# Token and channel mixer behind a retention block: two transposes moved to the crossbar, a last chain cut in halves, GpSimd scaling a few tiles, and a new fixed order of the work

## The chip, the core and the metric

The kernel runs on one core of a Trainium2 chip. A core has a matrix engine (TensorE, PE in the profile; its weight loads are shown apart as PEld), a vector engine (VectorE, DVE), a scalar engine (ScalarE, ACT), a general engine (GpSimd, POOL) and an engine that here only issues transfers (SyncE, SP). The engines run their own instruction streams and wait for one another through semaphores. Products land in eight banks of PSUM; ACT and DVE empty them into the on-chip memory (SBUF). Time is the device time of one launch in microseconds (us). The kernel before took 187.42 us, the median of 3 runs (186.85 to 187.65).

## The reference

Two parts follow each other. The first is a recurrence over 768 steps for 4 batches of 8 heads with 64 channels:

```python
gamma = 1.0 - 2.0 ** (-5.0 - np.arange(H))          # one decay for each head
scale = 1.0 / np.sqrt(D)
for t in range(S):
    state = gamma[None, :, None, None] * state + np.einsum('bhd,bhe->bhde', k[:, :, t], v[:, :, t])
    y[:, :, t] = scale * np.einsum('bhd,bhde->bhe', q[:, :, t], state)
```

With heads side by side, y is x of the second part, 4 x 768 x 512. That part mixes along the 768 steps and then along the 512 channels:

```python
xt = x.transpose(0, 2, 1)
h  = np.maximum(xt @ w_tok1, 0.0) @ w_tok2           # 768 -> 256 -> 768
u  = x + h.transpose(0, 2, 1)
h2 = np.maximum(u @ w_ch1, 0.0) @ w_ch2              # 512 -> 1536 -> 512
return u + h2
```

Inputs and output are 32-bit floats; the kernel multiplies in 16 bits.

## The kernel before

The 768 steps are cut into 6 chunks of 128, the 8 heads into 4 pairs. The recurrence is computed by chunk: inside a chunk as masked scores times v, between chunks through a state of 64 x 64 for each head.

`front(b, p)` (L501) does one pair of one batch up to u. GpSimd issues the loads of q, k and v (L489, L492), which change type on the way; k of the very first pair comes by SP instead (L492, tile `us`) and in 32 bits. Then:

- `decayed` (L524 to L538) scales k by a factor for each position, one instruction for each head of the pair, on ACT or DVE; for batches 2 and 3 it does the same with q.
- `turn` (L540 to L570) brings k and q to channels on the rows. In mode `t` PE transposes six chunks of 128 x 128 (L554) and one engine copies the bank out; in mode `w` PE does it head by head on half the columns of its array (also L554) and DVE scales on the way out; in mode `x` SP issues one crossbar transpose from SBUF to SBUF (L544).
- PE makes the state products of five chunks (L586) into one bank. DVE takes the first out as it is (L596) and chains the other four (L598). The chained states U are scaled into `cross`, one instruction for each head (L603 to L620).
- PE makes the scores (L637), DVE multiplies them with the causal mask into `am` (L648), PE multiplies `am` with v (L668) and q with `cross` into the same bank (L694). ACT or DVE casts the result to 16 bits (tile `x`, L710).
- Token mixer: PE multiplies with the first weight (tile `wt` of 128x6x256, called wt1 here, L725), ACT or DVE applies the ReLU (L734), PE adds the product with the second weight (two tiles of 128x2x384, wt2, L745) to the bank that still holds x. That is u. It is cast to 16 bits (tile `u`) and kept in 32 bits (tile `X`), both by L710.
- u is turned too, in mode `t` by PE with a copy by ACT or DVE (L790 and L796) or in mode `x` by SP (L780).

The table `TURNS` holds the modes of k, q and u for the 16 pairs: `twt` for the 8 pairs of batches 0 and 1, `xxx` for those of batches 2 and 3.

`back(b)` (L807 on) is the channel mixer. `widen` (L824, batch 0) makes the 1536 hidden channels in the plain way. `widen7` (batches 1 to 3) cuts both operands in two by two blocks and makes the product from seven block products instead of eight (L893); ACT copies partial sums out (L904), DVE adds them up (L913) and applies the ReLU in place (L917, tile `h`, 54 times). `narrow7` does the second product likewise (L1043, L1053), with DVE adding the results to `X` (L1060) and SP or ACT storing rows of 512 columns (L1086); `narrow` (L969, L978, L984) does what is left of batch 3 in the plain way. For the block sums DVE prepares differences of the weights and of the operands (L1007 among others).

PE can treat its 128 x 128 array as a whole, or as halves by rows (scores, L637) or by columns (state products, L586; mode `w`, L554). Matmuls of the three kinds alternate in the order.

The order is written out: `ORDERED` is a string in which two characters of base 62 name one operation, 1296 of them, and `WAYS` is a string with the choice of engine for each operation that has one. `arrange` (L111) goes through this order with a cost model, but only to give the operations banks and buffers and to place a few multiplications by zero (L1168) where it expects PE to be idle at the start. The instructions of every engine, the transfers issued by GpSimd, SP and ACT among them, stand in that order. An engine takes its own in order, so an instruction that waits holds up all behind it on that engine.

Of the kernel before, what the change touches and what calls it, by code (L numbers as in the profile page):

```python
# [9 lines left out]
FP = mybir.dt.float32  # L10
F16 = mybir.dt.float16
AF = mybir.ActivationFunctionType
# [26 lines left out]
class Rings:  # L39
# [12 lines left out]
    def land(self, q, op, t):  # L52
        if q == "POOL":
            return 1470 if t < 4500 else 2100 if t < 17000 else 1700
        if op.dma[0] == 48:
            return 1300 if t < 115000 else 900
        return 900
# [49 lines left out]
INTO, OUT_OF = 92, 111  # L107
FREE = dict(PE=300, ACT=2500, DVE=900, POOL=900, SP=750)


def arrange(ops, BANKS, seq, ways):  # L111
# [82 lines left out]
    while left:  # L194
        moved = False
        wake = INF
        for e in ENGINES:
# [18 lines left out]
            if e == "PE":  # L216
                if o.tiled != tiled:
                    s_ = max(t, free[e] + (INTO if o.tiled else 0) + (OUT_OF if tiled == "high" else 0))
                tiled = o.tiled
# [39 lines left out]
    "0b05040a07000d0103020e060c1e0h1f1i0f1j1g1h0j08090g1t1k1x1s1l0i1O1m1w1P1n1v0l1Q1o1u1S1R1p1y1T0o1z1q1U1r1V221W"  # L259
    "230n2o1A1X242p1Y0m1C1Z2q26202s272r1B2t0k1D2Y252C2D2Z0q2F2u212H302v2G28312a2w292E0r2b2c1E2x2y0t2I2z1F2d342A35"  # L260
    "0p2B1J362e37380s2K1G2f2M2J392L1H2g3a0w2N321I1K2j332h2O0v2i1L3c2P4K0A2k3e3d3b2Q3f2m3h0u2R2T2l3g3i3k1M2U3m3j3l"
    "0z2V1N5j3n3C4L3y3o2S0y3z2W2n3p3A47483q2X0x3t5k3r493u3E3B0E3s3w3vac3xaf3F3GaM3HaN3DadaPaO0Dagaear4aaxah3IaQ0C"
    "3Jas3Mat4baR3Pb73Qb8b13Nau0B3Oavb24cawaD3KaJ0Gayb3aGb9aKazao0F3L4laLaH4oap4n0L4daq3R3TaI4eaA1a3VaBaS4H4GaT4f"
    "ai4maUaj0H4gaE4pak4I4hal4i4J1bbjamaFaVbkan1d3SaC0JbaaWbm3Ubbbo3Wb4aXaYbnb5bc1caZ4jbg0Nb0bd16bh3Xbi0K17b6be3Y"
    "bqbl18bf0I3Z4UbI40bObr19410R424k4Y4M5fbvbP4V4r4t4Nbw4q6p4sbx4X0M4u4Obz4v4Pby43154Wbs5Obp45bA4Q44bBbJ5gbt4w46"
    "4RbKbE4xbL4SbTbCbF4T4Z50bU4y5P0T5152bD4z5Q5l5U4A5m4B0O535V5h5W4CbX5n5X540Pc44DbM5o5ibY555Y5pbNc56mc85q5Z56bR"
    "bu6qc65r575R5Sc95t5sbS5T5a585vcd6n5ubV6r5wce605y5x5AchbQ5C6oc7bW5z5Bci5b0Q6s6Uc06t5D594E5c0U6ucmc17s6v6V5E6w"
    "12cn4F6xcfbZ5F0S617t62cg5G6y640W5J5H665dcj655K145I635e5Mck68670X5N69ca6bcl5L6a0Vcb6A6ccqcu6X6C6d6Y6DcNcc6Z6e"
    "cLcrcvcwcM6B6f6z6WczcscQcxcA6icRct707u6gcCcOcTcD6EcBcUcScycocEcJ806GcV6I6jd0716hcKcGd1cXcH81d26FcY6kdR116H72"
    "d3d4cW736Jd9cZ74d7dS13d5dT6KdWd8d6dU7y7vda757zdX6L7AdbcFcPdZ767Bdcdhe0dY7w6Mde7C0Z7xdie1e683djcI7De3dfe76N6l"  # L270
    "e4dk78dV77dAdd7cdoc2dB6Q7bcp6OdC7982dpdFe5dq6RdDdldG7adrdIdEdsdm7e7gdJdHdt6S86dn84dydK7d7f87dzdP850Y886PdMdL"
    "89ey7hdu8adQe26TdNdv7ieWdg8yeu7j7EdwbGez8bc3eUeX7kev8B7Gew8C7l7K7FeDeQ8zeFdOdxeE7I8A7oeV7meGeHex7peJeS8c7reR"
    "7qeAeI7J7nf1eB8D96eK7M7O7HeMeLbHeZeNf27L7Nf0eC8e107Pe8f37Q8i99f58ff48h7R9a8g8dee9be97Secf697ef9E7TeY8jea8k7U"
    "7Wf7ed8m7V8Eeg9c7XeTej9H7Z9d8F7Y8l9eeh8G9f8Hf898ekeieb8nen8I8of9el9g8J9h8peoemfc8Mep8q8Keq8O8L8r8Qfg8P8s8uer"
    "fx8t8Nfh9kfdfyfi8v9nflfjfCfmfz9mfD8Sfofe8wfO9lfpfF9F8R9ofvfGfA8U9G8Tfn9ifffE8VfqfMfwg58xfH8Wfs9IfN9Kft9jfJ9J"
    "8X9Lfkg6fKfQ9MfP8Ygaetfug7fRgbfT9N9qgdfU9O9p9PeO9r8Zg8gegc9Q90fW9t9s92fX9ufVgfgk91g3fY93ghfIg4g0fBgi949vglg1"
    "gD9w9SgEg2fSgmgg9R9UgIgn9xg9fZgFgJ9Tgr9y9VgLgsgtfrgGgMgKgu9z9W9XgN9ZgvgSgogwgTgBa19AgxgOgCgPfLgp9YgyhChIhEa0"
    "hGgza2gjhNhDhHgQa3gqgHhLhOa4hg9BhRhM9DhFa5hPhJa6hifbgYhSgRhrgAhQhha8hUhTa9hkhsabgUhvgVgZa7h095hK9Ch3hlh1hjfa"
    "hmh4gWePhphnh2h5hqhogXh7h6hth8hVh9huhwhchxhyhahYi2hZiAhbi3ijaai4hdi7ikhei0ilesi8i5iohAi9hzipiahWimhfiqhXi1ir"
    "ibiHisicihiTitiiieivifiRiwiCiBj8iSiFiYiDiGiWiUhBiyi6iIiXidjaixiziJiZjfiKj0kEiPiMj1iQj6iNj3jpj2j9j4koj7jdjbjq"  # L280
    "jrinjejwjujsjgjvkMkNkpjhjciEjxiVjtjniLjyjKiujojEigjik6jFjzjkjjkqjAjlkFkOkwk2kPkQkGjBk3k7kriOjCkRksjmkbk4jDkt"
    "j5kcjGkdjHjLkHkIkfkejIjPkSkujMjJkvjRjNkTk5khjQkgjSjTkijVkjjUkJkxkmjWjYjOkKk8jXkLkyjZkzk0k9kAk1kBkkkakCklkDkn"
)
WAYS = (
    "000000000000000000000000000000000000000000000000000000000000000000000000000010000000000000000000000000000010"
    "010100000000000000000000000001010000000100000000000000000000000000000000000100000000000010000000000010000000"
    "000101010000000000000000000000000000000010100000000000000000000000000000001000000000000000000000000000010100"
    "000000000000001000000000000000000001010110000000000000000000000000000000010000000000000000000000000000000000"
    "000000000000000000000000000000010010000000000000000000000000000000000000000000000000000000000000000000000000"
# [11 lines left out]
def kernel(  # L301
# [104 lines left out]
    def emit():  # L406
        for h in range(H):
            nc.vector.memset(lgs[:, h:h + 1], math.log(1.0 - 2.0 ** (-5.0 - h)))
# [792 lines left out]
```

## Time and profile before

| | before |
|---|---|
| time, median of 3 runs | 187.42 us (186.85 to 187.65) |
| time of the profiled execution | 186.83 us |
| its span | 185.0 us |
| granted clock of PE (1 is full) | 0.996 |
| PE busy | 177.1 us |
| PE's weight loads busy | 134.6 us |
| DVE busy | 170.2 us |
| ACT busy | 133.4 us |
| POOL busy | 53.6 us |

The span is what the profile sees, from the first instruction to the last; the time of the same execution is 1.8 us longer. In groups of instructions a row gives line, engine, operation, output and input by the program's names, the shape (partitions x elements), the count, then after the bar the busy time in us and the mean in ns of one, and last the idle time of the engine ahead of them with what ended most of it. In the chain of work that ended last, a row gives the start, the length, the engine and what it did; the chain is followed backwards from the last instruction, at each step to what released it or to the instruction ahead on the same engine. In the rows of transfers stand the tile, the queue, the count, the size of one and the median us from issue to landing.

### The profile page before, as it was taken

Reading aid. Unit: us, or ns where it says so; the run is one execution under the profiler, and the core shown is the slowest. Engines: PE = TensorE matmul, PEld = TensorE weight load, DVE = VectorE, ACT = ScalarE, POOL = GpSimd, SP = SyncE. Lnnn points to the kernel's source line nnn. Section 1 sums busy time; section 2 is a strip of 40 time slices with the busy share of each in tenths; the row PEclk is TensorE's granted clock in tenths of the full one; section 3 lists DMA queues with packets and bytes.
Section 4 is the critical chain, followed back from the end, with each engine's and each line's share of the span. In section 5 each row is a group of like instructions: output and inputs, shape, how many; then the busy total and the mean of one; then the engine's idle time right before and its main releaser. Section 6 shows DMA issues by size and latency. Waiting matters only on the chain.

```text
span 185.0 us, 5291 instructions
## 1 busy us (share of the span) xinstructions
PE 177.1 (96%) x2089; PEld 134.6 (73%) x2089; DVE 170.2 (92%) x466; ACT 133.4 (72%) x304; POOL 53.6 (29%) x63
## 2 busy tenths in 40 slices
PE   7788899999999999999999999999999999999991
PEld 3456788656689988866668898667679986567881
DVE  4599799859999999999999999999999999999992
ACT  5689698469789899999999697898864416552120
POOL 8994786355424609704220020000000000000000
PEclk9999999999999999999999999999999999999998
DMA  6999999999999999999999995027002444500035
GB/s 117 143 160 176 199 170 198 194 189 206 167 157 154 121 156 123 156 148 185 146 233 161 190 138 100 4 43 198 3 0 40 123 143 174 225 0 0 4 142 198
DMA packets 92248, 24.91 MB, mean 135 GB/s; under 512 B 81984, under 2 KB 89280, under 8 KB 92224
## 3 DMA queue, kind: packets, MB, share of 16 engines
q0 software_dynamic: 67728, 13.18, 89.8%
q1 hardware_dynamic: 23056, 9.11, 25.4%
q10 hardware_dynamic: 1440, 2.29, 3.3%
q8 instruction: 16, 0.26, 0.6%
q14 instruction: 8, 0.07, 0.1%
HBM read 26.74 MB, written 6.29 MB: 179 GB/s over the span
## 4 chain that ended last, share of the span: by engine, by line
PE 69%; DVE 16%; POOL 6%; DMA 5%; issue 2%; ACT 1%; POOLq 0%
PE bank L893 18%; PE bank L1043 11%; PE bank L824 9%; PE bank L1053 9%; DMA wt<-in_moe_w_tok_dram 5%; PE bank L745 5%; PE bank L725 4%; DVE X L1060 4%; DVE am L648 4%; DVE hs L1007 3%; PE bank L969 3%; DVE h L913 2%; POOL v L492 2%; PE bank L668 2%; PE bank L637 2%; PE bank L694 2%
## 5 line engine op out<-in xcount | busy, mean ns | idle before, releaser
L648 DVE TENSOR_TENSOR am<-bank,mask 128x384 f16<-128x384 f32 x64 | 32.9, 547 | 2.9 <-PE bank L637 2.8
L913 DVE TENSOR_TENSOR h<-bank,us 128x384 f16<-128x384 f32 x54 | 28.8, 551 | 0.6 <-PE bank L893 0.2
L904 ACT COPY us<-bank 128x384 f32<-128x384 f32 x50 | 23.3, 489 | 8.3 <-PE bank L893 6.4
L492 POOL DMA_DIRECT2D v<-in_v_dram x16 | 16.5, 1034 | 40.4 <-PE bank L694 25.7
L893 PE MATMUL bank<-hs,late 128*128 128x384 f16 x108 | 22.6, 326 | 0.0
L1033 ACT COPY us<-bank 128x256 f32<-128x256 f32 x30 | 10.7, 373 | 14.5 <-PE bank L1043 9.5
L1043 PEld LDWEIGHTS <-hs 128*128 128x128 f16 x198 | 18.5, 98 | 2.4
L893 PEld LDWEIGHTS <-late 128*128 128x128 f16 x144 | 13.2, 98 | 8.2 <-issue 0.4
L1060 DVE TENSOR_TENSOR X<-X,bank 128x256 f32<-128x256 f32 x44 | 17.7, 412 | 0.8 <-PE bank L1053 0.4
L1043 PE MATMUL bank<-wsum,hs 128*128 128x256 f16 x132 | 17.5, 273 | 0.0
L598 DVE SCALAR_TENSOR_TENSOR U<-U,gp,bank 128x64 f32<-128x64 f32 x64 | 16.8, 274 | 0.7
L710 ACT CAST u<-bank 128x384 f16<-128x384 f32 x31 | 14.6, 487 | 3.9 <-PE bank L745 3.3
L824 PE MATMUL bank<-uT,wc 128*128 128x384 f16 x96 | 16.9, 326 | 0.0
L492 POOL DMA_DIRECT2D k<-in_k_dram x15 | 15.4, 1033 | 4.9 <-DVE am L648 1.4
L710 ACT CAST x<-bank 128x384 f16<-128x384 f32 x30 | 14.1, 483 | 3.6 <-PE bank L694 3.4
L893 PE MATMUL bank<-uT,wc 128*128 128x384 f16 x72 | 16.4, 326 | 0.1
L616 ACT ACTIVATE cross<-U,gp 64x320 f16<-64x320 f32 x29 | 16.2, 559 | 0.4
L745 PE MATMUL bank<-h,wt 128*128 128x128 f16 x192 | 15.7, 219 | 0.3 <-DMA wt<-in_moe_w_tok_dram 0.3
L530 ACT ACTIVATE k<-k,gk 128x384 f16<-128x384 f16 x25 | 14.9, 617 | 1.4 <-DMA k<-in_k_dram 1.1
L840 ACT ACTIVATE h<-bank 128x384 f16<-128x384 f32 x24 | 10.6, 492 | 5.0 <-PE bank L824 4.8
L710 ACT COPY X<-bank 128x384 f32<-128x384 f32 x29 | 14.0, 492 | 0.0
L745 PEld LDWEIGHTS <-wt 128*128 128x128 f16 x192 | 12.3, 98 | 2.2 <-DMA wt<-in_moe_w_tok_dram 0.5
(91 smaller groups left out, 382.8 us busy)
## 6 DMA issues: line engine op xcount, KB each, us to landing
out_dram<-X SPq DMA_DIRECT2D x15, 256.0 KB, 3.1
q<-in_q_dram POOLq DMA_DIRECT2D x16, 192.0 KB, 8.4
v<-in_v_dram POOLq DMA_DIRECT2D x16, 192.0 KB, 7.3
k<-in_k_dram POOLq DMA_DIRECT2D x15, 192.0 KB, 7.9
wc<-in_moe_w_ch_dram POOLq DMA_DIRECT2D x5, 512.0 KB, 13.9
out_dram<-X ACTq DMA_DIRECT2D x8, 256.0 KB, 2.5
wc<-in_moe_w_ch_dram POOLq DMA_DIRECT2D x2, 256.0 KB, 10.6
us<-in_k_dram SPq DMA_DIRECT2D x1, 384.0 KB, 3.4
```

The source lines that it names most:

```text
L492: (nc.sync if hard else nc.gpsimd).dma_start(out=tile_of(s, [P, 2, NC, D], FP if hard else F16), in_=src.rearrange("h (c p) d -> p (h c) d ...
L598: nc.vector.scalar_tensor_tensor(out=u[:, c], in0=u[:, c - 1], scalar=gp[:, p:p + 1], in1=st, op0=ALU.mult, op1=ALU.add)
L648: nc.vector.tensor_tensor(am, SC[g].tile[:, :m * P].rearrange("p (i t) -> p i t", t=P), mask.to_broadcast([P, m, P]), ALU.mult)
L710: (nc.scalar.copy if e == "ACT" else nc.vector.tensor_copy)(tile(), t)
L745: nc.tensor.matmul(Y[j].tile[:, 2 * i * D:2 * (i + 1) * D], wt2[:, jt, t], H1.tile[:, jt], start=False, stop=(jt == NJ - 1), skip_group_ch ...
L824: nc.tensor.matmul(acc[:, :SH], wc1[:, ct, ft * P:(ft + 1) * P], UT.tile[:, ct, sh * SH:(sh + 1) * SH], start=(ct == 0), stop=(ct == NP - 1))
L893: nc.tensor.matmul(acc[:, :SH], left(ct), r[:, ct], start=first and ct == 0, stop=ct == C2 - 1, skip_group_check=True)
L904: (nc.scalar.copy if e == "ACT" else nc.vector.tensor_copy)(ks[:, j], R1.tile[:, :SH])
L913: nc.vector.tensor_tensor(h(m, sh), R.tile[:, :SH], KS.tile[:, j], ALU.add)
L1043: nc.tensor.matmul(acc_[:, lo], l[:, j], r[:, j], start=first and j == 0, stop=j == K2 - 1, skip_group_check=True)
L1053: nc.tensor.matmul(acc_[:, lo], l[:, j], r[:, j], start=first and j == 0, stop=j == K2 - 1, skip_group_check=True)
L1060: (nc.vector if e == "DVE" else nc.gpsimd).tensor_tensor(dst(), dst(), b_(), ALU.add)
```

## The change

Six things change in the code; the rest is the new order.

- `TURNS` has `twx` for the first two pairs of batch 1: their u goes through SP's crossbar transposes. The operations for PE's transposes and the copies out of the bank are gone for these two.
- GpSimd becomes one of the possible engines for scaling k (L533 of the changed kernel) and for scaling states (L620), in batch 0 alone. `WAYS` gives it four scalings of k and five of states.
- ACT becomes a possible engine for the first state out of the bank (L596 before) and for the ReLU in place behind the seven block products (L917 before). `WAYS` gives it 9 of the 16 and 21 of the 54.
- The last seven-product step of batch 3 (the blocks 2 and 3) makes its last chain, six matmuls of 256 columns, as two chains of six with 128 columns, each with its own addition and its own store. The stores of its rows are cut: row block 3 as a whole, the left half of block 2, and then two quarters.
- The factors for k and for q come from two separate operations, so that scaling k waits for fewer of them.
- The cost table of `arrange` has other numbers, and knows three kinds of tiling (`row`, `col`, `turn`) with a price for leaving each.

`ORDERED` and `WAYS` are new from end to end, with 1300 operations. Of the tables, one line of each is shown.

```diff
-            return 1470 if t < 4500 else 2100 if t < 17000 else 1700
+            return 1470 if t < 4500 else 2100 if t < 26000 else 1700
...
-INTO, OUT_OF = 92, 111
-FREE = dict(PE=300, ACT=2500, DVE=900, POOL=900, SP=750)
+CHANGE = {"": 92, "row": 110, "col": 100, "turn": 110}
+FREE = dict(PE=300, ACT=2100, DVE=900, POOL=900, SP=750)
...
-                    s_ = max(t, free[e] + (INTO if o.tiled else 0) + (OUT_OF if tiled == "high" else 0))
+                    s_ = max(t, free[e] + CHANGE[tiled])
...
 ORDERED = (
-    "0b05040a07000d0103020e060c1e0h1f1i0f1j1g1h0j08090g1t1k1x1s1l0i1O1m1w1P1n1v0l1Q1o1u1S1R1p1y1T0o1z1q1U1r1V221W"
+    "0d0106070c090e0b000g0308050a0f1g0h1h1k0l1i1l0i1j1U0j1v1V1u1Q1z1R1w0k1x1m1S1n1y1A0m1T1o1p0n1q25241r2r2q262u1s"
...
-    TURNS = "twt twt twt twt twt twt twt twt xxx xxx xxx xxx xxx xxx xxx xxx".split()
+    TURNS = "twt twt twt twt twx twx twt twt xxx xxx xxx xxx xxx xxx xxx xxx".split()
...
-        nc.scalar.activation(gk, lgs, AF.Exp, scale=-1.0)
-        nc.scalar.activation(gy, lgs, AF.Exp, bias=lnsc, scale=1.0)
-    g_op = prep("ACT", 380, emit, [lgs_op])
+    g_op = prep("ACT", 190, lambda: nc.scalar.activation(gk, lnG, AF.Exp, scale=away[:, MID:MID + 1]), [away_op, logs_op])
+    gy_op = prep("ACT", 190, lambda: nc.scalar.activation(gy, lgs, AF.Exp, bias=lnsc, scale=1.0), [lgs_op])
...
-                got.append(op(either(emit, ACT=(506, 610), DVE=(780, 860) if hard else (600, 690) if b == 0 else (262, 342)),
-                              [dep, g_op], [] if got else [dst], ([dst] if got else []) + [src],
+                got.append(op(either(emit, ACT=(506, 610), DVE=(340, 420) if hard else (600, 690) if b == 0 else (231, 312),
+                                     **(dict(POOL=pool(SH)) if b == 0 else {})),
+                              [dep, gy_op if tag == "q16" else g_op], [] if got else [dst], ([dst] if got else []) + [src],
...
-                    nc.vector.tensor_copy(u[:, 0], st)
+                    (nc.scalar.copy if e == "ACT" else nc.vector.tensor_copy)(u[:, 0], st)
...
-                        nc.vector.tensor_scalar(r, u, g, None, ALU.mult)
-                rs.append(op(either(emit, ACT=(455 + 115 * j, 555 + 40 * j), DVE=(465, 545)), [prev, cross_op] + rs, [] if j else [RS],
+                        (nc.vector if e == "DVE" else nc.gpsimd).tensor_scalar(r, u, g, None, ALU.mult)
+                rs.append(op(either(emit, ACT=(455 + 115 * j, 555 + 40 * j), DVE=(465, 545),
+                                    **(dict(POOL=pool(320)) if b == 0 else {})), [prev, cross_op] + rs, [] if j else [RS],
...
-                        nc.vector.tensor_scalar(h(m, sh), h(m, sh), 0.0, None, ALU.max)
-                    rel[i + m * M2, sh] = op(one("DVE", (180, 260), emit), [ad], [], [H2s[sh]])
+                            nc.scalar.activation(h(m, sh), h(m, sh), AF.Relu)
+                        else:
+                            nc.vector.tensor_scalar(h(m, sh), h(m, sh), 0.0, None, ALU.max)
+                    rel[i + m * M2, sh] = op(either(emit, DVE=(167, 250), ACT=act(SH, 0, 1)), [ad], [], [H2s[sh]])
...
+            if b == B - 1 and i1 == 3:
+                store(i1, slice(0, C), [y2])
+                store(i0, lo, [y11])
+                got = k4
+                for g in range(2):
+                    cols = slice(g * P, (g + 1) * P)
+
+                    def emit(cols=cols, left=lambda: HS.tile[:, 3], right=w(1, hi)):
+                        l, r = left(), right()
+                        for j in range(K2):
+                            nc.tensor.matmul(banks[0].tile[:, cols], l[:, j], r[:, j, cols], start=False, stop=j == K2 - 1,
+                                             skip_group_check=True)
+                    got = op(one("PE", (336, 500), emit), [sm[3], got] + cw, [], [ha, hb, HS, banks[0]])
+                    last = slice(N2 + g * P, N2 + (g + 1) * P)
+                    o12 = add(part(x0, last), lambda cols=cols: banks[0].tile[:, cols], [got] + xd, [X, banks[0]],
+                              dict(DVE=(200, 284)))
+                    store(i0, last, [o12])
```

Three places show what the new order does.

GpSimd at the start, from the middle of batch 0's loads. Each row is a line of the kernel and an instruction with output and input; the tiles end in a number that is not that of the pair. Before (`wt_79` is wt1, `wt_80` is wt2, `v_272` and `q_363` are v and q of pair 3):

```order
L492 DMA k_164<-in_k_dram 128x12x64
L489 DMA q_177<-in_q_dram 128x2x384
L492 DMA k_183<-in_k_dram 128x12x64
L492 DMA v_220<-in_v_dram 128x12x64
L472 DMA wt_79<-in_moe_w_tok_dram 128x6x256
L492 DMA v_272<-in_v_dram 128x12x64
L472 DMA wt_80<-in_moe_w_tok_dram 128x2x384 x2
L489 DMA q_363<-in_q_dram 128x2x384
```

And now (`wt_80` is wt1, `wt_81` is wt2, `q_265` and `v_412` are q and v of pair 3; `k_..<-k_..,gk` are scalings of k, `cross<-U` scalings of a state):

```order
L493 DMA k_178<-in_k_dram 128x12x64
L493 DMA v_198<-in_v_dram 128x12x64
L533 TENSOR_SCALAR k_22_218<-k_123,gk 128x6x64 x2
L493 DMA v_225<-in_v_dram 128x12x64
L490 DMA q_265<-in_q_dram 128x2x384
L473 DMA wt_80<-in_moe_w_tok_dram 128x6x256
L533 TENSOR_SCALAR k_23_294<-k_137,gk 128x6x64
L620 TENSOR_SCALAR cross_77<-U_254,gp 64x5x64
L473 DMA wt_81<-in_moe_w_tok_dram 128x2x384
L533 TENSOR_SCALAR k_21_378<-k_178,gk 128x6x64
L473 DMA wt_81<-in_moe_w_tok_dram 128x2x384
L493 DMA v_412<-in_v_dram 128x12x64
```

The q of pair 3 went from the last place to the one ahead of wt1, its v from behind wt1 to the last place, and five computing instructions stand ahead of that v.

PE where it first reads the last of these loads. Before, that is the q of pair 3, turned behind the last L745 of pair 0:

```order
L745 LDWEIGHTS wt_80
L745 MATMUL bank_420<-h_57_526,wt_80 128x128
L554 LDWEIGHTS q_363
L554 MATMUL bank_553<-ident_73,q_363 64x128
L554 LDWEIGHTS q_363
```

Now it is the v of pair 3, read by the state products (L588 of the changed kernel) behind the L728 (before: L725) of a pair:

```order
L728 LDWEIGHTS wt_80
L728 MATMUL bank_526<-x_53_487,wt_80 128x128
L588 LDWEIGHTS k_21_378
L588 MATMUL bank_544<-v_412,k_21_378 64x64
L588 LDWEIGHTS k_21_378
```

The first reader of the last load is a state product where it was a transpose, and pair 3's scores stand right behind it.

SP's first transfers. Before:

```order
L492 DMA us_85<-in_k_dram 128x12x64
L544 DMA_TRANSPOSE kT_1371<-k_23_1269 128x6x128
L544 DMA_TRANSPOSE qT_1509<-q_25_1480 128x6x128
L544 DMA_TRANSPOSE qT_1530<-q_24_1230 128x6x128
L544 DMA_TRANSPOSE kT_1556<-k_21_1451 128x6x128
L544 DMA_TRANSPOSE qT_1804<-q_25_1780 128x6x128
```

And now, with the two of u in batch 1 (`uT`, L783):

```order
L493 DMA us_86<-in_k_dram 128x12x64
L546 DMA_TRANSPOSE qT_1434<-q_25_1262 128x6x128
L783 DMA_TRANSPOSE uT_1458<-u_62_1125 128x6x128
L546 DMA_TRANSPOSE qT_1480<-q_24_1212 128x6x128
L546 DMA_TRANSPOSE kT_1517<-k_22_1240 128x6x128
L546 DMA_TRANSPOSE kT_1555<-k_23_1523 128x6x128
L783 DMA_TRANSPOSE uT_1458<-u_63_1360 128x6x128
L546 DMA_TRANSPOSE qT_1632<-q_25_1563 128x6x128
```

The two of u stand second and sixth among the transposes, between those of q and k of batch 2, of which there are no fewer than before.

137 lines of the change are left out of this document (72 added, 65 removed).

## The prediction

> **What bounds the kernel now.** I read first the page's busy times, then the chain that ended last in order of time, then one stretch of matmuls counted by form.
>
> ```profile
> span 185.0 us, 5291 instructions
> PE 177.1 (96%) x2089; PEld 134.6 (73%) x2089; DVE 170.2 (92%) x466; ACT 133.4 (72%) x304; POOL 53.6 (29%) x63
> ACT  5689698469789899999999697898864416552120
> ```
>
> The last row is ACT's busy tenths in 40 slices of the span. Two engines look full, PE and DVE. Which of them ends the others' waits decides what the change is worth, because it takes far more from DVE than from PE. The chain, piece by piece (start, length, what):
>
> ```profile
> 9.91 0.82 POOL wt L472
> ...
> 11.65 9.10 DMA wt<-in_moe_w_tok_dram
> ...
> 20.80 0.51 PE bank L745 x6
> 21.31 0.67 PE bank L725 x12
> ...
> 22.43 0.17 PE bank L668 x6
> ...
> 22.77 0.34 PE bank L745 x6
> 23.10 0.46 PE bank L554 x12
> 23.56 0.44 PE bank L745 x6
> ...
> 31.72 2.37 PE bank L824 x14
> ...
> 102.20 1.41 DVE hs L1007 x3
> ...
> 180.63 0.67 PE bank L1043 x6
> ...
> 181.32 0.42 DVE X L1060
> ```
>
> GpSimd issues loads until the second weight of the token mixer (wt2, 11.65) and the chain waits for its landing at 20.75. From 20.80 on PE pieces follow each other. The rows also give PE's rate: a 128-wide matmul takes 0.34/6 = 0.056 us, a 64-wide one 0.17/6 = 0.029, a 256-wide one 0.67/6 = 0.11. And they give the price of changing the array's tiling: the six L745 behind other full-array work take 0.34, the six right behind the q transposes on half columns (L554) 0.44, so a change costs 0.10.
>
> Between 86 and 119 us the chain runs through DVE. Is PE idle there? The groups of PE in 102 to 108:
>
> ```profile
> L1043 PE MATMUL bank<-wsum,hs 128*128 128x256 f16 x17 | 2.4, 273 | 0.0
> L1053 PE MATMUL bank<-wsum,h 128*128 128x256 f16 x12 | 1.6, 272 | 0.0
> L1043 PE MATMUL bank<-wc,hs 128*128 128x256 f16 x6 | 0.8, 273 | 0.0
> L1053 PE MATMUL bank<-wc,h 128*128 128x256 f16 x6 | 0.8, 272 | 0.0
> L1053 PE MATMUL bank<-wsum,hs 128*128 128x256 f16 x6 | 0.8, 272 | 0.0
> L668 PE MATMUL bank<-v,am 128*128 128x64 f16 x12 | 0.7, 193 | 0.0
> L694 PE MATMUL bank<-cross,qT 128*128 128x128 f16 x5 | 0.6, 219 | 0.0
> L637 PE MATMUL bank<-qT,kT 64*128 64x128 f16 x12 | 0.5, 218 | 0.0
> ```
>
> 47 x 0.11 + 12 x 0.029 + 5 x 0.056 + some 0.4 for the twelve scores = 6.2 us of matmuls in a 6 us stretch. PE is full there too. So my reading is: the start (to 20.8) is bound by loads issued by GpSimd, and everything behind it by PE, with DVE just keeping pace.
>
> **The change part by part.** All sums stand against the profiled execution, 186.83 us (span 185.0, so 1.8 around it). The median of the runs shown is 187.42, 0.6 above; the forecast is carried over to it at the end.
>
> Transposes by crossbar. Pairs 0 and 1 of batch 1 no longer turn u on PE: 12 matmuls of 128 columns go, two rows of 0.34: -0.67 us on the path. Their two copies out of the bank leave ACT or DVE, hidden beside PE. SP issues two more transposes:
>
> ```profile
> uT<-u SPq DMA_TRANSPOSE x8, 2.9
> kT<-k SPq DMA_TRANSPOSE x8, 5.0
> ```
>
> They land 3 to 5 us after issue. In the new order the second one stands on SP behind a k transpose of batch 2, and on PE some 9 us of matmuls stand between it and the first that reads it, two further pairs of the same batch among them. What hides it is this PE work. Cost 0. Were that cover gone, what it cost is at most the 5.0 of a landing.
>
> Fewer changes of tiling. Counted in the order of PE from the point where the last load of batch 0 is first read: 53 changes before, 46 now (scores and state products stand side by side three times, and more q transposes stand together). 7 x 0.10 = -0.7. From below: half of them fall in a wait, -0.35.
>
> The last chain in halves. Twelve matmuls of 128 columns for six of 256: 12 x 0.056 - 0.67 = 0.00. Behind it:
>
> ```profile
> L978 DVE TENSOR_TENSOR X<-X,bank 128x128 f32<-128x128 f32 x2 | 0.6, 279 | 0.0
> out_dram<-X SPq DMA_DIRECT2D x1, 256.0 KB, 2.0
> out_dram<-X SPq DMA_DIRECT2D x1, 64.0 KB, 1.6
> ```
>
> The last addition shrinks from 0.42 to 0.28, the last store (256 KB at 181.8) from 2.0 to 1.6; but it now waits for another store of 64 KB on SP, about 0.1. Together -0.4.
>
> Work moved off DVE. 21 of the 54 ReLU passes in place and 9 of the 16 first states go to ACT, ACT gives DVE six scalings of k and five casts of u:
>
> ```profile
> L917 DVE TENSOR_SCALAR h<-h 128x384 f16<-128x384 f16 x54 | 12.3, 259 | 0.1
> L596 DVE COPY U<-bank 128x64 f32<-128x64 f32 x16 | 3.4, 215 | 0.4 <-PE bank L586 0.3
> L530 ACT ACTIVATE k<-k,gk 128x384 f16<-128x384 f16 x25 | 14.9, 617 | 1.4 <-DMA k<-in_k_dram 1.1
> ```
>
> 21 x 0.23 + 9 x 0.21 and a few copies out, about 6 in: DVE loses some 4 us net. While PE is the bound that is worth nothing. A pass in place on ACT isn't in the trace; between the 0.26 of DVE and ACT's 0.62 for the same size with a scale, I take 0.5, nearer ACT's row. In the last ten slices ACT is busy for six tenths at most; 8 of the passes go there.
>
> The start. GpSimd's queue, where the change adds nine computing instructions:
>
> ```profile
> 0.84 0.46 POOL L422 IOTA us<- 128x384 f32 x1 [0.39 <-POOLq L1185]
> 8.84 1.07 POOL L492 DMA_DIRECT2D v<-in_v_dram  x1
> 9.84 0.89 POOL L472 DMA_DIRECT2D wt<-in_moe_w_tok_dram  x1
> ...
> 13.13 0.72 POOL L489 DMA_DIRECT2D q<-in_q_dram  x1
> q<-in_q_dram POOLq DMA_DIRECT2D x1, 192.0 KB, 4.6
> wt<-in_moe_w_tok_dram POOLq DMA_DIRECT2D x1, 384.0 KB, 8.7
> q<-in_q_dram POOLq DMA_DIRECT2D x1, 192.0 KB, 9.6
> ```
>
> The first load took 4.6 us from issue to landing, the q of pair 3 (13.13) 9.6: 5 us of queue. So the loads are bound by transfer, and an issue that comes later costs nothing until the queue is empty. The same loads stand ahead of the same last one, except that the last is now v of pair 3, not q. It lands when that q did, 13.13 + 9.6 = 22.7, if it is issued by 22.7 - 4.6 = 18.1. Five computing instructions stand ahead of it. No row shows one; between the IOTA's 0.46 (same engine and size, only writing) and the 1.07 of a load's issue I take 0.5, since IOTA is the nearest. Adding the issues at 0.72 to 1.07, I get the v issued at about 15.7: a margin of 2.4 us. Cost of the nine: 0, hidden by that queue.
>
> But the order has a price. The token mixer's first weight (issued 9.84, landing 18.5) now lands behind that q as well, 1 us later, at 19.5. Counted in the order and priced with the rates above, PE has 8.2 us of work behind it at 23.10 before, and 7.4 when the v lands and is read at 22.85 now. So it stands 0.8 - 0.25 = 0.55 us behind: +0.55.
>
> New waits. In 102 to 108 PE has none left to lose. The new order may bring one: pair 3 gets both scaled states from GpSimd, where ACT and DVE shared them, in front of the products that read them. Laid out with 0.5 each they are ready 0.2 us before PE comes to them; at 1.07 each PE would wait about 0.9. Bounds 0 and 0.9; I take 0, by the same IOTA row.
>
> Sum: -0.67 - 0.7 + 0.0 - 0.4 + 0.55 + 0 = -1.2, so 185.6 for the profiled execution, and 187.42 - 1.2 = 186.2 against the median: faster by 0.65%. About 0.5% (0.94 us) is what a measurement of this kernel can tell from no change, so this is just over it.
>
> **The rivals.** *DVE is the bound after all.* The chain's DVE stretch and 92% speak for it; against it the count in 102 to 108, and this row, by which a weight load (98 ns) is hidden under a 256-wide matmul (0.11 us):
>
> ```profile
> L1043 PEld LDWEIGHTS <-hs 128*128 128x128 f16 x198 | 18.5, 98 | 2.4
> ```
>
> Then the 4 us that DVE loses are a gain, less what falls outside its full stretch (about half): 1.2 + 2 = 3.2 us, 184.2. The Trainium skill, Perfetto Trace Analysis, section Identifying the Most-Contended Engine, would have it so: it says to judge TensorE not by matmul busy time but by how busy the weight loads are, and here these are at 73%, under DVE's 92%; by that rule the time would be this 184.2.
>
> *GpSimd holds the loads back (slower).* One computing instruction of length T costs nothing up to the margin: 5 (T - 0.5) - 2.4 for the v, and 2 (T - 0.5) - 0.2 for pair 3's states. From T = 1.18 on the two reach 2.2 us, which turns the forecast into a slowdown of over 0.5%; at T = 1.25 they are 2.7: 188.9. For it: nothing prices them, they read as well as write, and they wait for k and the states while loads queue behind. Against: IOTA's 0.46. The Trainium skill, GPSIMD Engine Reference, section Instruction dispatch, says that the first call of a freshly loaded GpSimd kernel waits about 6 us for its code; by that, as an estimate, the v would be issued at 21.7, 3.6 too late, and the time would be 189.8. No run here shows it so far.
>
> *The order doesn't hold what it counts on.* ACT and DVE are so full between 50 and 86 that small lateness on either (a pass in place at 0.62, a crossbar transpose behind loads) reaches PE. An extra 1.2 us takes the gain: 187.4, no change.
>
> **How the numbers follow.** Forecast 0.45, its own range 185.4 (less DVE work also spares some small waits) to 187.1 (waits of 0.9): faster 0.32, same 0.13. DVE as the bound 0.13, all faster. GpSimd 0.22: slower 0.19, same 0.03, since a T just under 1.18 only eats the gain. Order 0.20: same 0.14, slower 0.04, faster 0.02. So faster 0.47, same 0.30, slower 0.23. The range reaches from DVE's 184.2 to GpSimd's 188.9.
>
> **What would show it.** Right: wt1 is first read near 19.5, PE has no wait over 0.2 after 23, GpSimd's instructions take near 0.5, the end is some 0.4 nearer the last matmul. Wrong: GpSimd's instructions over 1 us; a first one with 6 us of idle behind it; PE waiting for ACT's ReLU; or a gain of 3 us with PE's own count unchanged.

## The result and the profile after

The changed kernel took 192.07 us, the median of 6 runs (190.98 to 192.79), beside 187.22 us of the kernel before (6 runs, 186.85 to 187.78). The ratio is 1.0249, with a 95% interval of 1.0218 to 1.0280: slower by 4.9 us, where 186.2 was forecast and the range ended at 188.9. The profiled execution took 192.49 us.

The page of the changed kernel, busy times first, then slices of 4.8 us:

```profile
span 190.7 us, 5316 instructions
...
PE 178.4 (94%) x2088; PEld 135.4 (71%) x2088; DVE 168.5 (88%) x442; ACT 135.2 (71%) x318; POOL 64.8 (34%) x72
...
PE   7766896999999999999999999999999999999993
...
POOL 8999999936446400962008020000000000000000
PEclk9999998899999999999999999999999999999999
```

The span is 5.7 us longer, but PE is busy only 1.3 us longer. GpSimd went from 53.6 to 64.8 us, and is full through the first eight slices, where it had been at three to eight tenths from the fourth on. PE has gaps up to the seventh slice, which the kernel before had up to the fifth. From the eighth slice on both look alike. So most of the loss lies in the first 35 us.

What GpSimd's computing takes, in the groups of that engine:

```profile
L620 POOL TENSOR_SCALAR cross<-U,gp 64x320 f16<-64x320 f32 x5 | 5.6, 1114 | 0.4
L533 POOL TENSOR_SCALAR k<-k,gk 128x384 f16<-128x384 f16 x4 | 5.0, 1249 | 0.2
L423 POOL IOTA us<- 128x384 f32 x1 | 0.5, 455 | 0.4 <-POOLq L1211 0.4
```

A scaling of k takes 1.25 us and one of a state 1.11, not the 0.46 of the IOTA of the same size. All nine are 10.6 us on the engine that issues the loads. In order of time:

```profile
8.03 1.04 POOL L493 DMA_DIRECT2D v<-in_v_dram  x1
9.16 2.48 POOL L533 TENSOR_SCALAR k<-k,gk 128x384 f16<-128x384 f16 x2
11.59 1.07 POOL L493 DMA_DIRECT2D v<-in_v_dram  x1
12.66 0.72 POOL L490 DMA_DIRECT2D q<-in_q_dram  x1
13.35 0.88 POOL L473 DMA_DIRECT2D wt<-in_moe_w_tok_dram  x1
14.24 1.28 POOL L533 TENSOR_SCALAR k<-k,gk 128x384 f16<-128x384 f16 x1
...
19.56 1.03 POOL L493 DMA_DIRECT2D v<-in_v_dram  x1
...
27.97 2.39 POOL L620 TENSOR_SCALAR cross<-U,gp 64x320 f16<-64x320 f32 x2
```

And what PE waited for (total, times, longest):

```profile
PE bank L697 <- POOL cross L620: 2.8, 3, 2.2
PE bank L558 <- DVE qT L566: 1.5, 1, 1.5
...
PE bank L558 <- POOL k L533: 1.0, 1, 1.0
PE bank L588 <- DMA v<-in_v_dram: 0.6, 1, 0.6
```

The two lists belong together. GpSimd's first two scalings (pair 1) end at 11.64, and PE turns that k at 11.69. Its third (pair 2) stands behind three load issues and ends at 15.52; PE turns that k at 15.58, after a wait of 1.5 that the view puts down to an older DVE instruction. The two states of pair 3 end at 30.36, and PE reads them at 30.41 after 2.2 us. DVE had these states ready for scaling at 26.8; GpSimd was issuing loads until 27.9, and then took 2.39 for the two. In PE's order of time these are the rows, with the two state products that matter for the loads:

```profile
10.37 0.35 PE L588 MATMUL bank<-v,k 128*64 128x64 f16 x10 [0.60 <-DMA v<-in_v_dram]
11.69 0.51 PE L558 MATMUL bank<-ident,k 128*128 128x128 f16 x6 [0.98 <-POOL k L533]
15.58 0.51 PE L558 MATMUL bank<-ident,k 128*128 128x128 f16 x6 [1.52 <-DVE qT L566]
24.79 0.35 PE L588 MATMUL bank<-v,k 128*64 128x64 f16 x10
30.41 0.27 PE L697 MATMUL bank<-cross,qT 128*128 128x128 f16 x2 [2.19 <-POOL cross L620]
```

The 0.6 us for a v is at 10.37: that load was issued at 4.12, ahead of every scaling. The last v, issued at 19.56 and so 4 us later than I counted on, landed at 24.23, and PE came to it at 24.79 without a wait.

One thing more went wrong just behind that last wait. In stretches of 1 us the columns are PE busy, PEld, DVE, ACT and POOL, then the granted clock of PE:

```profile
28.00:29.00 1.00, 0.22 (x4) 0.10 (x2) 1.00 (x3) 0.38 (x1) 1.00 (x1) 1.00 1.32 166
29.00:30.00 1.00, 0.00 (x0) 0.00 (x0) 0.48 (x3) 0.00 (x0) 0.91 (x2) 1.00 2.02 138
...
32.00:33.00 1.00, 1.00 (x12) 1.00 (x11) 0.00 (x0) 0.97 (x3) 1.00 (x2) 0.50 1.04 115
33.00:34.00 1.00, 1.00 (x12) 1.00 (x10) 0.56 (x1) 0.00 (x0) 1.00 (x2) 0.50 1.38 176
34.00:35.00 1.00, 1.00 (x13) 1.00 (x11) 0.10 (x1) 0.38 (x1) 1.00 (x3) 0.50 1.14 185
```

PE stands empty from 28.2 to 30.4, and from 31.6 to 35.0 it runs at half its clock: 12 or 13 matmuls in a us. That is another 1.6 us.

### The profile page after: what moved, and what is told of

Same layout as the page of the kernel before. It is cut to its first block, busy times and chain, and to the rows that moved or that the text cites. A ratio compares the mean times of both kernels' runs of the same rounds, so it can differ in the third digit from the quotient of the medians.

```text
span 190.7 us, 5316 instructions
## 1 busy us (share of the span) xinstructions
PE 178.4 (94%) x2088; PEld 135.4 (71%) x2088; DVE 168.5 (88%) x442; ACT 135.2 (71%) x318; POOL 64.8 (34%) x72
## 4 chain that ended last, share of the span: by engine, by line
PE 77%; POOL 11%; DVE 3%; DMA 3%; issue 2%; ACT 2%; POOLq 0%
PE bank L896 20%; PE bank L1049 15%; PE bank L1059 11%; PE bank L827 8%; PE bank L748 5%; PE bank L728 5%; DMA k<-in_k_dram 3%; PE bank L975 3%; POOL k L533 3%; PE bank L640 3%; PE bank L671 2%; POOL cross L620 2%; PE bank L697 2%; POOL v L493 2%; POOL q L490 2%
## 5 line engine op out<-in xcount | busy, mean ns | idle before, releaser
L907 ACT COPY us<-bank 128x384 f32<-128x384 f32 x49 | 22.3, 483 | 6.5 <-PE bank L896 3.1
L1039 ACT COPY us<-bank 128x256 f32<-128x256 f32 x31 | 11.5, 374 | 12.5 <-PE bank L1049 12.1
L1049 PEld LDWEIGHTS <-hs 128*128 128x128 f16 x192 | 18.0, 98 | 2.1
L1066 DVE TENSOR_TENSOR X<-X,bank 128x256 f32<-128x256 f32 (+1 forms) x45 | 17.6, 406 | 0.9 <-PE bank L1059 0.7
L713 ACT COPY X<-bank 128x384 f32<-128x384 f32 x32 | 15.6, 494 | 1.6 <-DVE X L1066 1.6
L748 PE MATMUL bank<-h,wt 128*128 128x128 f16 x192 | 15.7, 222 | 0.1
L618 ACT ACTIVATE cross<-U,gp 64x320 f16<-64x320 f32 x24 | 13.4, 559 | 2.4 <-DVE U L600 2.1
L713 ACT CAST u<-bank 128x384 f16<-128x384 f32 x26 | 12.4, 482 | 2.6 <-PE bank L748 2.5
L748 PEld LDWEIGHTS <-wt 128*128 128x128 f16 x192 | 12.9, 99 | 1.8
L728 PE MATMUL bank<-x,wt 128*128 128x128 f16 x192 | 14.0, 225 | 0.0
L896 PEld LDWEIGHTS <-wc 128*128 128x128 f16 x108 | 9.9, 98 | 5.5
```

Of the source, the lines that this page charges most:

```text
L713: (nc.scalar.copy if e == "ACT" else nc.vector.tensor_copy)(tile(), t)
L728: nc.tensor.matmul(acc[:, jt * P:(jt + 1) * P], wt1[:, i, jt * P:(jt + 1) * P], X16.tile[:, i].rearrange("p h d -> p (h d)"), start=(i == ...
L748: nc.tensor.matmul(Y[j].tile[:, 2 * i * D:2 * (i + 1) * D], wt2[:, jt, t], H1.tile[:, jt], start=False, stop=(jt == NJ - 1), skip_group_ch ...
L896: nc.tensor.matmul(acc[:, :SH], left(ct), r[:, ct], start=first and ct == 0, stop=ct == C2 - 1, skip_group_check=True)
L907: (nc.scalar.copy if e == "ACT" else nc.vector.tensor_copy)(ks[:, j], R1.tile[:, :SH])
L1049: nc.tensor.matmul(acc_[:, lo], l[:, j], r[:, j], start=first and j == 0, stop=j == K2 - 1, skip_group_check=True)
```

## The experiments

Ratios are against the kernel before, run on the same chip beside each experiment. "The base" below is the first experiment's kernel.

**Nine off GpSimd** (`e1`, repeated as `h2`). The four scalings of k go to ACT, the states to ACT and DVE, by `WAYS`; one pair of neighbours in `ORDERED` is exchanged for it (here and in `e2`):

```diff
 WAYS, batch 0
-"...0020000000000000", "001001220000010000200000000000100000001001200000010000020000000000000000001000020000000000220..."
+"...0000000000000000", "001001000000010000000000000000100000001001000000010000000000000000000000001000000000000000100..."
```

> The changed kernel with its nine computing instructions taken from GpSimd: the four scalings of k and four of the five of states go to ACT, one state to DVE, as in the kernel before (one pair of neighbours in the order is exchanged for it). Theory A (GpSimd's instructions of 1.1 to 1.25 us hold up the loads behind them and the states): the whole loss of 4.9 us goes, and what the prediction counted beside it shows, so 185.5 to 187. Rival B (the new order of the start is slow by itself, with or without GpSimd): 190 or more. Rival C (half and half): 188 to 189.

> The first experiment again, beside the others on this chip: 186.0 as before, ratio 0.993 to 0.997. Should it come out at 187 or more here, the differences of the last four runs to it were those of chips.

Measured: 186.01 us, ratio 0.9947 (0.9926 to 0.9968), and on another chip 185.84, ratio 0.9950 (0.9925 to 0.9975). Theory A holds: without the nine instructions the changed kernel is faster than the one before, by 0.5%, where the prediction had 0.65%. The nine cost 5.6 us (1.0249 - 0.995 = 3.0%). This kernel beats both.

**Part of them off** (`e2`, `e3`), the same edit for the four of k, or for the five states, alone.

```diff
 WAYS, batch 0, only k off / only states off
-"...0020000000000000", "001001220000010000200000000000100000001001200000010000020000000000000000001000020000000000220..."
+"...0020000000000000", "001001000000010000200000000000100000001001000000010000020000000000000000001000000000000000220..."
+"...0000000000000000", "001001220000010000000000000000100000001001200000010000000000000000000000001000020000000000100..."
```

> Only the four scalings of k go from GpSimd to ACT; the five states stay on GpSimd. Theory A: loads are held up by one state instead of five instructions, but PE still waits for the last states (2.8 us in the profile of the changed kernel): 187.5 to 189.5. Rival B: 190 or more. If the scalings of k cost nothing, it stays at 192.

> Only the five scalings of states go from GpSimd to ACT and DVE; the four of k stay on GpSimd. Theory A: the loads are still held up by four instructions of 1.24 us, and the waits for states go: 188 to 190. Rival B: 191 or more. If the states are all of it: 186 to 187.

Measured: 187.56 us, ratio 1.0040 (1.0026 to 1.0055), with the states left on GpSimd, and 188.20, ratio 1.0080 (1.0043 to 1.0118), with k left there. Over the base the states alone cost 0.9% and k alone 1.3%: 2.2% or some 4 us, and both together 5.6. Two things fit the rest. Each makes the other later: in `e2` PE waits 1.0 us for a state, in the changed kernel 2.2. And the low clock of PE shows in none of the 10 executions of `e2`, in 2 of the 5 of `e3` and in 6 of 10 of the changed kernel.

**The same nine in the old order** (`e4`): GpSimd added as an engine as in the change, and in `WAYS` of the kernel before the same nine.

```diff
+                                     **(dict(POOL=pool(SH)) if b == 0 else {})),
...
-                        nc.vector.tensor_scalar(r, u, g, None, ALU.mult)
+                        (nc.vector if e == "DVE" else nc.gpsimd).tensor_scalar(r, u, g, None, ALU.mult)
```

> The kernel before, with the same nine scalings (by pair and head) given to GpSimd at their places in its own order, nothing else changed. Theory A: GpSimd's 10.6 us of computing delay the loads behind them in that order too, so 190 to 193. Rival B (it is the new order): within 1 us of the kernel before, 187 to 188.2.

Measured: 191.81 us, ratio 1.0264 (1.0246 to 1.0283). So it is these instructions and not the new order. PE's waits in it:

```profile
PE bank L557 <- POOL k L532: 2.7, 3, 1.1
PE bank L696 <- POOL cross L619: 1.7, 3, 0.8
```

**Short ones on GpSimd** (`h1`), at their places and with their waits. Each sets its piece to zero and scales only the first chunk; the other five of k, or four of a state, are left out of the computation:

```diff
+                        c_ = slice(0, 1 if e == "POOL" else NC)
+                        if e == "POOL":
+                            nc.gpsimd.memset(t, 0.0)
-                        (nc.vector if e == "DVE" else nc.gpsimd).tensor_scalar(t, src.tile[:, j], g[:, h:h + 1], None, ALU.mult)
+                        (nc.vector if e == "DVE" else nc.gpsimd).tensor_scalar(t[:, c_], src.tile[:, j, c_], g[:, h:h + 1], None, ALU.mult)
...
```

> The changed kernel with its nine scalings left on GpSimd at their places and with their waits, but short: each sets its piece to zero and scales only the first chunk of it, so five of six chunks of these k (four of five of these states) are left out of the computation. Theory A (what failed in the forecast is only the length T, 1.24 and 1.09 us where 0.5 was taken): at T of 0.5 to 0.6 the time falls back to that of the kernel with nothing on GpSimd or a little over it, 186.0 to 187.0. Rival (any computing between loads on GpSimd holds the loads back, by its waits and not its length): 189 or more.

Measured: 188.94 us, ratio 1.0103 (1.0078 to 1.0127), between the two. But the experiment missed its length. GpSimd's groups in it:

```profile
L626 POOL TENSOR_SCALAR cross<-U,gp 64x64 f16<-64x64 f32 x5 | 2.2, 448 | 0.5
L625 POOL MEMSET cross<- 64x320 f16 x5 | 1.8, 364 | 0.2
L536 POOL TENSOR_SCALAR k<-k,gk 128x64 f16<-128x64 f16 x4 | 1.8, 446 | 0.4
L535 POOL MEMSET k<- 128x384 f16 x4 | 1.8, 446 | 0.0
```

Zeroing and scaling the first chunk together still take 0.8 to 0.9 us, so this is the point 0.9 and not 0.5. It shows that length counts (188.9 at 0.9, 191.5 at 1.1 to 1.25 on the same chip) and that 0.9 already costs 3 us, below the 1.18 that the prediction gave as the point of decision. In its profile PE has no wait for a k from GpSimd any more, and 0.6 us for a state. Not all of the 3 us is the queue: set against the base's second profile, 1.1 is there by 20 us, where this execution had a slow start, 0.9 comes with the states of pair 3, and 1.1 with four ReLU on DVE at 97 us. Whether 0.5 would have been free stays open; since 64 elements take 0.45 and 384 take 1.25, no scaling of this size could be that short.

**Zeros in the wait** (`f4`), to see whether the low clock comes from PE standing empty:

```diff
-                if i in banks or i == 7 and t < F_ON:
+                if i in banks or i == 7 and t < 31000:
...
+            if o.n == 208:
+                for _ in range(12):
+                    nc.tensor.matmul(spare[:, :384], zero[:, :P], zero, start=True, stop=True)
```

> The changed kernel with 12 multiplications by zero (2.0 us of work that nobody reads, in a spare bank) put on PE where it waits 2.3 us for pair 3's states. Theory A (the clock of 0.5 that PE shows from 31.7 to 35 us in the profile comes from its standing empty just before): the clock stays at 1.0 in every execution and the time falls by about 1.5 us from 192.1, to 190.3 to 191.0. Rival (the clock has nothing to do with that wait): some executions still show a clock of 0.98 to 0.99, and the median stays within 0.4 of 192.1.

> The changed kernel again on this chip: 191 where PE's clock stays at 1.0 and 192.5 where it falls to 0.98 or 0.99 in the mean. If the low clock comes from the 2.3 us for which PE stands empty at 28 us, part of these executions show it, and none of those of the kernel with nothing on GpSimd.

Measured: 191.74 us, ratio 1.0226 (1.0169 to 1.0284), and the changed kernel again 191.48, ratio 1.0254 (1.0210 to 1.0297). In the profile of `f4` the wait is filled and the clock stays at 1.00 from 26 to 36 us, but one of its four executions had a mean clock of 0.991, and its median is within 0.4 of the changed kernel's. By the expectation that is the rival's side. But the edit does more than fill the wait: it also keeps the bank of the zeros (7) from other work until 31 us of `arrange`'s time instead of 21. Set against `h3`'s profile, the L728 at 22.5 us starts within 0.1 us of its place and the one ahead of the wait 0.57 us late (28.45 against 27.88); the last matmul then ends 0.9 us earlier (187.3 against 188.2). So the edit seems to lose time ahead of the wait and to gain more behind it, and the median can't decide. What the executions do show together: a mean clock of 0.98 or 0.99 stood in 6 of the 10 of the changed kernel (191.4 to 193.1 us, against 191.0 to 191.7 for the others), in 1 of the 22 of the base, and in 5 of 6 of the next experiment, whose longest wait is 2.7 us. Others stand between: 2 of 5 in `e3` (longest wait 1.5), 3 of 6 in `f3` (1.7), 3 of 12 in `g3` (1.1), none of 5 in `h4` (1.6). The low clock mostly goes with long waits; that filling this one wait removes it isn't shown.

**Old start, new rest** (`f1`), then with one q later (`g3`): `ORDERED` and `WAYS` joined from both kernels at the first matmul of the channel mixer.

```diff
 ORDERED, WAYS
-all 1300 operations as in the changed kernel
+194 operations as in the kernel before, then the others as in the changed kernel
+g3: and L556 for q of pair 1 of batch 1, with its copy, behind the eighth L827
```

> The order of the kernel before, with its engines, up to the first matmul of the channel mixer (194 operations, about 31 us), and the order of the changed kernel from there; no computing on GpSimd. Theory A (the new order of the start costs PE some 0.9 us even without GpSimd's computing, which is the difference of PE's lag at 25 us between the kernel before and the first experiment, 14.9 and 15.8 us): 0.9 below the first experiment's 186.0, so 184.8 to 185.4. Rival (the new start costs nothing, the two starts are alike): 185.8 to 186.3.

> As the experiment with the old start and the new rest, but the q of pair 1 of batch 1, whose load the old start issues behind two weights, is turned on PE behind seven more products of the channel mixer, where its load has landed. Theory A (the 2.8 us wait for that q was all that was wrong with the splice, and the new start by itself costs 0.9): 185.0 to 185.6. Rival (the new start costs nothing): 185.8 to 186.4. Above 187: the two halves of the orders don't fit in other places either.

Measured: 191.37 us, ratio 1.0204 (1.0154 to 1.0254), and 188.09, ratio 1.0050 (1.0025 to 1.0076). Neither expectation was met in `f1`, and `g3` came out by its third, above 187: the halves don't fit. `f1` shows it in one row of PE's timeline, a wait for a q whose load the old start issues behind two weights:

```profile
34.83 0.53 PE L556 MATMUL bank<-ident,q 128*64 128x128 f16 x12 [2.66 <-DMA q<-in_q_dram]
```

Whether the new start is slower by itself has to be read from the traces: the first matmul of the channel mixer began at 31.66 us in the kernel before, and at 32.80 and 31.41 in two profiles of the base. The start of one kernel varies by 1.4 us, so the +0.55 of the prediction can't be told. The variation comes from PE's own speed in the first 10 us: the twelve transposes of a q (L556) that begin at 6.14 us in both profiles of the base take 0.85 us in the first and 0.53 in the second.

**One part alone in the old order** (`f2` last chain, `f3` crossbar, `h4` ReLU on ACT), the code of the change for that part, with its operations placed by me.

```diff
 f2
-            p3 = chain(lambda: HS.tile[:, 3], w(1, hi), [sm[3], k4] + cw, False, True)
+                    got = op(one("PE", (336, 500), emit), [sm[3], got] + cw, [], [ha, hb, HS, banks[0]])
...
 f3
-    TURNS = "twt twt twt twt twt twt twt twt xxx ..."
+    TURNS = "twt twt twt twt twx twx twt twt xxx ..."
 h4
-                    rel[i + m * M2, sh] = op(one("DVE", (180, 260), emit), [ad], [], [H2s[sh]])
+                    rel[i + m * M2, sh] = op(either(emit, DVE=(180, 260), ACT=act(SH, 0, 1)), [ad], [], [H2s[sh]])
```

> The kernel before with the last chain in halves, two additions of 128 columns and the stores in pieces, and nothing else. The prediction: 0.4 below the kernel before, so about 186.45 beside its 186.86. Rival (the end hangs on the last store's fixed time, not on the size): no change, 186.7 to 187.0.

> The kernel before with u of the first two pairs of batch 1 turned by SP's crossbar instead of PE, and nothing else: 12 matmuls and two copies less. The prediction: 0.67 below the kernel before, so about 186.2. Rival (the crossbar's transfers land late or hold back the k transpose behind them on SP): 186.9 or more.

> The kernel before with the same 21 ReLU passes in place on ACT, and nothing else. The prediction (PE is the bound and DVE only keeps pace): within 0.4 of the kernel before. Rival, DVE as the bound: half of the 5 us that DVE loses is gained, 184.5. Third: ACT's 0.52 instead of 0.25 us comes late for the product that reads it, slower by 0.5 or more.

Measured: 188.18 us, ratio 1.0053 (1.0031 to 1.0075); 189.57, ratio 1.0132 (1.0081 to 1.0182); 190.64, ratio 1.0185 (1.0155 to 1.0216). All three slower, each for a reason of its own. In `f2` the last PE work ends at 181.8 and the span at 186.6, 4.8 us later, against 3.75 before: five stores were issued within 1.3 us at the end, where I had put them, and each took 2.2 to 2.8 us to land. In `f3` the crossbar's transfers of u took long, and PE waited; here the rows of PE's waits and of that tile's four issues from 50 to 100 us, of which the first two are the added ones (8.8 and 8.5):

```profile
PE bank L893 <- DMA uT<-u: 1.7, 1, 1.7
```

```profile
DMA to landing us min/median/max: 4.4/7.6/8.8
```

In `h4` PE waits for ACT, which does a pass in 0.52 us where DVE took 0.26 and is itself nearly full there, as the third expectation had it:

```profile
PE bank L893 <- ACT us L904: 1.4, 3, 0.9
...
PE bank L1046 <- ACT us L1036: 0.6, 1, 0.6
```

**One part undone in the base** (`g1` u turned on PE again, `g2` one last chain, `g4` the 21 ReLU back on DVE).

```diff
 g1
-    TURNS = "twt twt twt twt twx twx twt twt xxx ..."
+    TURNS = "twt twt twt twt twt twt twt twt xxx ..."
 g2
-                    got = op(one("PE", (336, 500), emit), [sm[3], got] + cw, [], [ha, hb, HS, banks[0]])
+            p3 = chain(lambda: HS.tile[:, 3], w(1, hi), [sm[3], k4] + cw, False, True)
...
 g4, WAYS of the 21 passes: ACT
-...1001001...
+...0000000...
```

> The first experiment (the changed kernel with nothing computed on GpSimd, 186.0) with u of the first two pairs of batch 1 turned on PE again: 12 matmuls of 128 columns and two copies by ACT come back, PE's a few products behind the place of the crossbar's transposes. Theory A (PE is the bound and the new order hides the crossbar's 5.7 us): slower by 0.67 to 0.9, so 186.7 to 186.9. Rival (PE has slack there, or the transposes fill waits): within 0.3 of 186.0.

> The first experiment (186.0) with the last chain whole again, one addition of 256 columns and one store of 256 KB for the last rows. Theory A (the shorter last addition and store are worth the 0.4 of the prediction): 186.4. Rival (the end costs the same, since stores pile up there): within 0.2 of 186.0.

> The first experiment (186.0) with all 54 ReLU passes in place on DVE again: 21 more passes of 0.25, 5.3 us more for DVE and 21 fewer for ACT. Theory A (PE is the bound and DVE keeps pace): 186.0 to 186.8. Rival, DVE as the bound: half or more of the 5.3 us comes back, 188.5 to 191.

Measured: 188.54 us, ratio 1.0081 (1.0050 to 1.0111); 187.11, ratio 0.9992 (0.9970 to 1.0015); 189.28, ratio 1.0117 (1.0084 to 1.0150). Beside the base's 0.995, the crossbar is worth 1.3%, the halves 0.4% and the ReLU on ACT 1.7% in this order, each within some 0.4% either way. `g1` and `g2` came out above both of their expectations; `g4` came out as its rival had it. The first includes a wait of 0.6 us for ACT's copy, which my placing made. In the last PE waits for DVE, at four places:

```profile
PE bank L1059 <- DVE hs L1013: 1.8, 4, 0.9
```

So every part pays in the order that was made for it, and none of the three in the old one.

## Why the prediction was wrong

**The step that failed: "Cost of the nine: 0, hidden by that queue".** It failed in three ways.

- The length. Between the IOTA's 0.46 and a load's issue of 1.07 I took 0.5 "since IOTA is the nearest". An IOTA only writes. The scalings took 1.25 and 1.11, above both ends: neither row bounded an instruction that reads as well.
- Who waits. I priced what stands behind these instructions on GpSimd, the loads, and found a margin of 2.4 us. The margin didn't hold, and yet the loads cost PE nothing that can be seen: the last v was issued at 19.56 instead of 15.7, past the limit of 18.1, and landed 1.5 us behind the 22.7, but PE was late for it by other waits. (In the base's second profile it landed at 22.20, and PE read it at 22.45.) So this delay was covered by another one. What I didn't price is who waits for the results. PE turns the scaled k of pairs 1 and 2, and GpSimd delivers one of them behind three load issues. Set against the base's second profile, which has a quick start like that of the changed kernel, the latter is 1.43 us later when it turns the k of pair 1, and 1.47 more at that of pair 2, of which it makes up 0.53 by 27 us.
- The states of pair 3. The bounds were 0 and 0.9; it was 2.3 us. GpSimd came to them late from all that stood ahead (ready at 26.8, begun at 27.97), and two of them took 2.39 in a row.

The three places in the base's second profile, to be set beside the 11.69, 15.58 and 30.41 above:

```profile
10.26 0.51 PE L558 MATMUL bank<-ident,k 128*128 128x128 f16 x6
12.68 0.51 PE L558 MATMUL bank<-ident,k 128*128 128x128 f16 x6
25.70 0.27 PE L697 MATMUL bank<-cross,qT 128*128 128x128 f16 x2
```

Together 1.43 + 1.47 - 0.53 + 2.33 = 4.7 us by the time of the last states. The low clock added 1.6 in the profiled execution. A last 0.9 came later: at 100.8 us four in-place ReLU on DVE took 1.82 us, and 1.29 in the base, and PE waited for what followed. In the other direction 0.3 was made up at 60 us. That is all of the 6.9 us between the two profiles' last matmuls. The 1.82 stands in the second profile of the changed kernel too, and 1.81 in that of `h1`; why these ReLU take longer there isn't shown.

**The rival "GpSimd holds the loads back"** had the engine, the sign and even the T (1.25), but gave 188.9 instead of 192.1. Of its two terms at that T, some 1.3 each, the states came true and more (2.3), while the wait for the last v didn't appear; neither k nor the clock was in it. Its point of decision, 1.18, was too high: at 0.9 the kernel was 1% slower than before. Its chance of 0.22 was too small: an operation that no row shows, on the engine that the start hangs on, should have weighed most. The 6 us for a first call of a GpSimd kernel, from the Trainium skill (GPSIMD Engine Reference, section Instruction dispatch), didn't appear: the first two scalings started 0.1 us behind the load ahead of them and took 2.48 together. The same page, in its section Engine selection, calls GpSimd roughly line-rate for one input; here a scaling of 128x384 took 1.25 us on GpSimd, 0.62 on ACT and 0.39 on DVE, so the measurement decides.

**The rest of the sum** came out: -1.2 was forecast without any cost of the nine, and the base measures -0.5% (0.9 to 1.1 us). Its second profile ends 1.2 us earlier than that of the kernel before (183.8 against 185.0). In part that is luck: undone one at a time, three of its parts cost 2.4, 0.8 and 3.1 us, where the terms were 0.67, 0.4 and nothing, so the sum is right while its terms are not.

- Crossbar -0.67: right in sign, and more in the base (1.3%, part of it my own wait). "Cost 0" held there: the second of the two landed at 74.1 us, and PE reads it first at 77.2. Alone in the old order the landing took up to 8.8 us, not "at most the 5.0 of a landing", and it cost. The 5.0 was a median and no upper end: in the kernel before one crossbar transpose of u already took 6.8.
- Tiling -0.7: with the time lost at each change added up, the changes behind 25 us took about 5.4 us before and about 4.9 and 4.7 in the two profiles of the base, so -0.5 to -0.7.
- The last chain -0.4: from the last matmul to the end of the span it is 3.75 us before and 3.13 to 3.16 in the base and in the changed kernel, so -0.6; undoing it cost 0.4%.
- Work moved off DVE, taken as worth nothing while PE is the bound: true as a difference to the kernel before, wrong as a reading. The new order needs that freed time: given back, it costs 1.7%. So in this order DVE binds as well as PE. The size was off too: DVE's busy time fell by 1.7 us (170.2 to 168.5), not by "some 4".
- "PE has no wait over 0.2 after 23" was wrong (2.2 at 28); that the end is some 0.4 nearer the last matmul was right, and wt1 was first read at 22.1 instead of 19.5 (19.7 and 21.1 in the two profiles of the base).

## What to carry to other kernels

Price an instruction that is new to an engine from a row with the same operands, or not at all: a row that only writes is no lower neighbour of one that reads and writes, and where none exists its range has to reach well past the rows at hand. On a queue that both issues and computes, ask two questions of each new instruction: what stands behind it, and who waits for its result, which now comes behind everything ahead of it. And a part of a hand-made order can't be judged alone: all three parts that paid in the new order lost time in the old one.

## What the hardware showed

- PE's granted clock fell to 0.50 for 3.4 us in both profiles of the changed kernel, near the end of a stretch of 2.0 to 2.2 us in which PE was empty: 31.6 to 35.0 with PE empty from 28.2 to 30.4, and 30.5 to 33.9 with PE empty from 28.7 to 30.8. In 6 of its 10 executions the mean clock was 0.98 or 0.99. The Trainium skill, TensorE: Matmul & The Clock Gate, section on the HAM clock gate, has half clock after an idle window of about 3.4 us that runs freely; the length of the low stretch fits one such window, while the empty time before it was shorter than one.
- In-place ReLU on DVE (128x384, 16 bits) took 0.26 us at most in the 27 cases of the changed kernel in which GpSimd did nothing at that time, and 0.55 to 0.79 in 3 of the 6 in which GpSimd was issuing a load; in the kernel before none of 48 beyond 0.26, and 0.68 in 1 of 6. The four that came together, from the changed kernel and from the base:

```profile
100.81 1.82 DVE L923 TENSOR_SCALAR h<-h 128x384 f16<-128x384 f16 x4
```

```profile
94.66 1.29 DVE L923 TENSOR_SCALAR h<-h 128x384 f16<-128x384 f16 x4
```

  The Trainium skill, SBUF — State Buffer, describes a port pair that DVE's fast modes and GpSimd take in turn, the loser waiting for the whole instruction. These rows agree with it; that the port is the cause wasn't tried.
- A scaling of k on GpSimd took 0.45 us for 64 elements in each partition (`h1`) and 1.25 for 384 (the changed kernel).
